# Float64 clamp on GpSimd and a shifted order of weight narrowing in a fused attention, rational layer and soft mixture kernel

## The chip, the cores and the metric

The kernel runs on one core of a Trainium2 chip, in one launch. The metric is the device time of an execution in microseconds (us). TensorE (PE) multiplies matrices; VectorE (DVE), ScalarE (ACT) and GpSimd (POOL) work elementwise; SyncE (SP) starts most of the transfers.

## The reference

Three layers follow each other. Attention works in chunks of 32 queries that see 16 keys to the left, 8 to the right and 8 memory slots. Its result, 3072 tokens by 512, goes through a rational layer and then through a soft mixture of 8 experts with 4 slots each:

```python
def _moe_ref(x, w_in, w_out, a, b):
    h = x @ w_in                                   # 512 -> 2048
    P = a[0] + a[1]*h + a[2]*h**2 + a[3]*h**3
    Q = 1.0 + abs(b[0])*abs(h) + abs(b[1])*h**2
    return (P / (Q + 1e-06)) @ w_out               # 2048 -> 512

def _moe2_ref(x, phi, w1, w2):
    logits = x @ phi                               # 32 slots
    d = softmax of logits over the tokens
    slot_out = relu((d.T @ x) @ w1[e]) @ w2[e]     # for each expert
    c = softmax of logits over the slots
    return c @ slot_out
```

The weights w_in and w_out arrive as float64 and are narrowed to float32 on the chip.

## The kernel before

The tokens are taken in six blocks of 512, and the 2048 hidden columns in eight steps of 256, so there are 48 steps, numbered k. In step k PE makes h for step k+1 (`h_part`, L380): in block 0 with plain float32 matmuls, later with a split of both operands into two parts. The elementwise chain of a step is: ACT takes |h| (L607) and h squared (L608) from PSUM, DVE adds them to the denominator Q (L609), ACT makes a3*h + a2 (L610), DVE goes on to the cubic with two passes that read h from PSUM (L619, L620). ACT makes 1/Q approximately by Ln and Exp (L624, L625). One step later POOL multiplies Q with this reciprocal (`refine`, L585), and DVE closes the Newton correction (L632, L633). The product is written into a buffer that L609 of the later step has just read, so it starts behind that L609. The result is turned on PE (L405) and multiplied with a small matrix wp (L398) to get the logits; copies are made by ACT (L406).

wp is phi times w_out, and it is made from eight pieces of w_out transposed, one per step: `narrow_w_turned` narrows piece i, `wp_sum` multiplies it (PE L483, ACT L485, PE L488, ACT L489). w_in comes in eight pieces also, narrowed by `narrow_w_in`. Pieces lie in buffers of the pool "g" (four buffers, shared with the gathered results `gts` of a block), so a load waits until an older piece was narrowed. `f64_narrow` does one piece of 128 x 1024 words in four passes: ACT scales the low words (L303), DVE clamps the high words (L304), ACT scales them (L305), DVE merges both (L307). All sixteen pieces are narrowed in the prologue and in block 0. `narrow_rows` does the same for other rows of w_out in later blocks with code of its own.

What order rules: in the prologue (up to `start.close()`) the order of PE, ACT, DVE and POOL is that of the list `pre`. After that a planner orders each engine's instructions by the order of writing, by its costs and by when their inputs are due; the list `ord0` gives the order of writing in a step of block 0, `ord` in later blocks. In the lists "s" narrows a w_in piece, "n" a w_out piece, "z" is `wp_sum`, "i" and "o" load pieces, "at" is a slice of the next block's attention, and the digit is the distance from the step's number. `issue_after(x)` keeps the planner from putting what it encloses ahead of x on x's engine; it waits for nothing.

Of the kernel before, what the change touches and what calls it, by code (L numbers as in the profile page):

```python
# [12 lines left out]
AF = mybir.ActivationFunctionType  # L13
ALU = mybir.AluOpType
# [5 lines left out]
def float_of_bits(u):  # L20
    return struct.unpack('<f', struct.pack('<I', u))[0]


KN = {
    'loads': "q0 q1 v0 i0 v1 c0 i1 o0 q2 v2 o1".split(),
    'pre': "f10 A A f5 B B A A A A B B A A B B A A A A s B B B B A A f2 A B B A s A B B A f2 B s B B B c f4 t t n n".split(),
    'pre2': "i2 o2 i3".split(),
    'ord0': "at a1 z0 s2 h0 d1 at t o3 i4 n1 at a2 y h1 p0 at p1 at at".split(),
    'ord': "at a1 h0 d1 at t a2 y x2 h1 p0 p1 x1 at x3 at at r".split(),
    'ordl': "a1 h0 d1 t a2 x2 h1 p0 p1 x1 x3 r".split(),  # L30
}

# [14 lines left out]
def tile_chunk_attention__rational__soft_moe(  # L47
# [16 lines left out]
    PE, ACT, DVE, POOL, SP = nc.tensor, nc.scalar, nc.vector, nc.gpsimd, nc.sync  # L64

    NPAIR, P, HP, _ = qw.shape
# [5 lines left out]
    NE, _, EFF = w1.shape  # L72
# [8 lines left out]
    NSTEP = NF // 2  # L81
# [4 lines left out]
    QC = 1.0 + 1e-6  # L86
    LN_SHIFT = 52
    LOW = 7.4 / 2.0 ** 32
    F64_HI = float_of_bits((1150 << 20) | 0xFFFFF)
# [22 lines left out]
    def bank(shape):  # L112
        return ps_m("m", shape)
# [160 lines left out]
    def constants():  # L274
        ACT.activation(ctab[:, 4:6], ctab[:, 4:6], AF.Abs)
        root, over = ctab[:, 7:8], run[:, 0:1]
        DVE.tensor_scalar(root, ctab[:, 5:6], 1e-37, None, ALU.max)
        ACT.activation(root, root, AF.Ln)
        ACT.activation(root, root, AF.Exp, scale=0.5)
        DVE.reciprocal(over, root)  # L280
        DVE.scalar_tensor_tensor(root, over, ctab[:, 5:6], root, ALU.mult, ALU.add)
        DVE.tensor_scalar(root, root, 0.5, None, ALU.mult)
        yield
# [7 lines left out]
    a0, a1, a2, a3 = (ctab[:, n:n + 1] for n in range(4))  # L291
# [4 lines left out]
    def f64_narrow(dst, src):  # L296

        lo, hi = src[:, :, :, 0], src[:, :, :, 1]
        f = hi.bitcast(F32)
        ACT.activation(lo, lo, AF.Copy, scale=LOW)  # L303
        DVE.tensor_scalar(f, f, -F64_HI, F64_HI, ALU.max, ALU.min)  # L304
        ACT.activation(f, f, AF.Prelu, scale=2.0 ** -112, alpha=-(2.0 ** 32))  # L305
        yield
        DVE.scalar_tensor_tensor(dst, hi, 3, lo, ALU.logical_shift_left, ALU.bitwise_or)  # L307
        yield
# [3 lines left out]
    win, w_f, st = {}, {}, {}  # L312
# [7 lines left out]
    def load_w_turned(i):  # L320
        t = p_g("g", [P, NC, 2 * P, 2], U32)
        for o in (slice(0, NC // 2), slice(NC // 2, NC)):
            SP.dma_start(out=t[:, o].rearrange("p c f w -> p c (f w)"), in_=w_turned[i, :, o])
        stage_out[i] = t

    def narrow_w_in(i):
        if i < NSTEP // 2:
            t = p_win("win", [P, 1024])
        else:
            if i % 2 == 0:  # L330
                st["x"] = p_x("x", [P, 2048])
            t = st["x"][:, 1024 * (i % 2):1024 * (i % 2) + 1024]
        w_f[i] = t.rearrange("p (c f) -> p c f", c=NC)
        yield from f64_narrow(w_f[i].bitcast(U32), stage_in.pop(i))

    def split_w(i):
        f = w_f.pop(i)
        wh, wl = win[i] = [p_win("win", [P, NC, 2 * P], F32R) for _ in range(2)]
        ACT.activation(wh, f, AF.Copy)
        DVE.tensor_tensor(wl, f, wh.bitcast(F32), ALU.subtract)  # L340
# [3 lines left out]
    def narrow_w_turned(i):  # L344
        wos[i] = scratch[i % 3].rearrange("p (c f) -> p c f", c=NC)
        yield from f64_narrow(wos[i].bitcast(U32), stage_out.pop(i))

    def load_rows(i):
        rows_of[i] = p_x("x", [P, 2, DM, 2], U32)
        SP.dma_start(out=rows_of[i].rearrange("p c f w -> p c (f w)"), in_=w_out[i])  # L350
# [145 lines left out]
    def load(what):  # L496
# [12 lines left out]
        elif kind == "o":  # L509
            load_w_turned(n)  # L510

    def convert(what):
        kind, n = what[0], int(what[1])
        if n < NSTEP:
            for _ in {"s": narrow_w_in, "n": narrow_w_turned, "z": wp_sum, "i": load_w_in, "o": load_w_turned}[kind](n) or ():
                pass

    new_xt(0)
    for what in KN["loads"]:
        load(what)  # L520
    gens = {"A": attention(0, after=NPAIR), "B": attention(1, lambda shape: p_T("T", shape), after=NPAIR),
            "s": narrow_w_in(0), "n": narrow_w_turned(0), "t": narrow_w_in(1), "c": constants()}
    for what in KN["pre"]:
        if what[0] == "f":
            busy(int(what[1:]))
# [16 lines left out]
    def slice_(n=1):  # L542
        for _ in range(n):
            if state["att"] is not None:
                try:
                    next(state["att"])
                except StopIteration:
                    state["att"] = None
# [33 lines left out]
    def refine(k, out=None):  # L582
        t, q, w = late[k]
        near[k] = out = q if out is None else out
        POOL.tensor_tensor(out, q, w, ALU.mult)  # L585

    late, near, behind, narrowing = {}, {}, {}, {}
    act = {}
# [1 line left out]
    def run_step(kk, what):  # L590
        b, i = divmod(kk, NSTEP)
        live, nxt = kk < total, kk + 1
        pb_, pi_ = divmod(kk - NSTEP, NSTEP)
        if what == "at":
            slice_()
        elif what in ("h0", "h1"):
            if nxt < total:
                if what == "h0":
                    if nxt % NSTEP == 0:
                        while state["att"] is not None:  # L600
                            slice_()
                    hs[nxt] = ps_h("h", [P, 2, BLK]) if nxt < total - 1 else [ps_h("h", [P, BLK]), bank([P, BLK])]
                h_part(nxt, hs[nxt], int(what[1]))
        elif what == "a1" and live:
            hh = hs[kk]
            s, t, y = p_S("S", [P, 2, BLK]), p_T("T", [P, 2, BLK]), p_S("S", [P, 2, BLK])
            ACT.activation(s, hh, AF.Abs, scale=b0)  # L607
            ACT.activation(y, hh, AF.Square, scale=rb1)  # L608
            DVE.scalar_tensor_tensor(s, y, QC, s, ALU.add, ALU.add)  # L609
            ACT.activation(t, hh, AF.Identity, bias=a2, scale=a3)  # L610
            act[kk] = s, t, y
        elif what == "d1":
            if live:
                s, t, y = act[kk]
                hh = hs.pop(kk)
            if kk - 1 in late and kk - 1 not in near:
                refine(kk - 1, y if nxt < total else None)
            if live:
                DVE.tensor_tensor(t, t, hh, ALU.mult)  # L619
                behind[kk] = DVE.scalar_tensor_tensor(t, t, a1, hh, ALU.add, ALU.mult).ins  # L620
        elif what == "a2" and live:
            s, t, _ = act.pop(kk)
            w = p_S("S", [P, 2, BLK])
            ACT.activation(w, s, AF.Ln, scale=2.0 ** -LN_SHIFT)  # L624
            st["exp"] = ACT.activation(w, w, AF.Exp, bias=ex_b, scale=-1.0).ins  # L625
            late[kk] = t, s, w
        elif what == "t":
            if kk - 1 in late:
                t, q, w = late.pop(kk - 1)
                e = near.pop(kk - 1)  # L630
                with tc.issue_after(behind[kk]) if kk in behind else nullcontext():
                    DVE.scalar_tensor_tensor(t, t, a0, w, ALU.add, ALU.mult)  # L632
                    st["t"] = DVE.scalar_tensor_tensor(t, e, 2.0, t, ALU.subtract, ALU.mult, reverse0=True).ins  # L633
                gt_tile[kk - 1] = t
        elif what == "y":
            if 0 <= kk - 6 < NSTEP:
                with tc.issue_after(st["exp"]):
                    split_w(kk - 6)
        elif what == "r":
            for n, at in ROWS.items():  # L640
                if kk == at[0]:
                    load_rows(n)
                    narrowing[n] = narrow_rows(n)
                for m in at[1:]:
                    if kk == m:
                        next(narrowing[n])
        elif what[0] == "x":
            n = int(what[1])
            if kk >= NSTEP and pi_ == (1, 2, 2)[n - 1]:
                (soft1, soft2, soft3)[n - 1](pb_)  # L650
        elif what[0] == "p":
            for k in LATER[i]:
                if 0 <= kk - k < total:
                    post(kk - k, int(what[1]))
        elif b == 0 and what[0] in "snwzio" and len(what) == 2:
            convert(what[0] + str(min(i + int(what[1]), NSTEP)))
# [56 lines left out]
    for kk in range(total + 4):  # L713
        b, i = divmod(kk, NSTEP)
# [138 lines left out]
    for b in range(NBLK):  # L853
        for half in range(2):
# [11 lines left out]
            for m in range(2):  # L866
                n = TT * b + 2 * half + m
# [67 lines left out]
```

## Time and profile before

| | us |
|---|---|
| median of 3 runs | 577.9 |
| lowest and highest | 576.36 and 578.36 |
| the profiled execution | 577.91 |
| its span in the trace | 575.8 |

The median is read against itself: runs differ by some 2 us. The profiled execution is as long as the median, and its span leaves out 2.1 us around it. All times in the trace count from the span's start. The prologue reaches to about 31 us, block 0 from the first L607 at 38.68 to the ninth at 133.26, the other five blocks to about 500 us, and the experts and the output fill the rest.

### The profile page before, as it was taken

How to read it: one execution, taken by the hardware profiler on the slowest of the kernel's cores; microseconds unless marked ns; L12 is line 12 of the kernel's file. 1: busy time of each engine (PE TensorE's matmuls, PEld its weight loads, DVE VectorE, ACT ScalarE, POOL GpSimd, SP SyncE). 2: the span in 40 equal slices, each digit the busy share in tenths (PEclk: the TensorE clock that was granted, in tenths of full speed). 3: DMA queues.
4: the chain of work that ended last, by engine and by line, in shares of the span. 5: the costliest groups of instructions: out<-in, count | busy, mean ns of one | idle time of the engine just before them, and what ended most of it. 6: DMA issues, size and time to landing. Idle time of an engine off the chain costs nothing.

```text
span 575.8 us, 13647 instructions
## 1 busy us (share of the span) xinstructions
PE 540.6 (94%) x5874; PEld 362.1 (63%) x5874; DVE 456.3 (79%) x572; ACT 427.9 (74%) x551; POOL 122.2 (21%) x66
## 2 busy tenths in 40 slices
PE   6799897999999999999999999999999999999991
PEld 6644443557767767677766777776768767643351
DVE  3759988989898999979899799898898978831042
ACT  1489896897978999779787888896888978721132
POOL 0001111213221322313231313132223322300000
PEclk8799898999999999999999999999999999999996
DMA  8997854301125315341432335304349374799948
GB/s 319 361 382 256 279 189 162 137 12 56 56 76 183 129 56 183 115 170 36 161 111 74 114 107 184 110 12 174 110 145 372 106 252 150 268 392 410 409 173 357
DMA packets 28139, 105.80 MB, mean 184 GB/s; under 512 B 3376, under 2 KB 3504, under 8 KB 27056
## 3 DMA queue, kind: packets, MB, share of 16 engines
q1 hardware_dynamic: 26928, 100.74, 48.1%
q0 software_dynamic: 1152, 4.19, 1.8%
q8 instruction: 46, 0.75, 0.5%
q14 instruction: 13, 0.11, 0.0%
HBM read 94.44 MB, written 10.49 MB: 182 GB/s over the span
## 4 chain that ended last, share of the span: by engine, by line
PE 56%; DVE 15%; ACT 14%; DMA 8%; issue 4%; POOL 1%; ACTq 0%; SPq 0%; DVEq 0%; POOLq 0%
PE h L380 28%; DMA g<-in_w_turned_dram 5%; PE m L405 4%; PE m L458 4%; ACT S L607 3%; PE lg L398 3%; ACT S L608 3%; ACT g L406 3%; DVE T L619 3%; PE h L796 2%; PE m L228 2%; DVE T L620 2%; PE lg L833 2%; DMA g<-in_moe_w_in_dram 2%; DVE T L632 2%
## 5 line engine op out<-in xcount | busy, mean ns | idle before, releaser
L380 PE MATMUL h<-xt,win 128*128 128x512 f32 x1012 | 268.5, 414 | 0.7 <-DVE T L620 0.6
L380 PEld LDWEIGHTS h<-xt,win 128*128 128x128 f32 x1012 | 184.1, 188 | 50.9 <-issue 12.3
L585 POOL TENSOR_TENSOR S<-S,S 128x1024 f32<-128x1024 f32 x46 | 112.2, 2440 | 335.1 <-DVE S L609 282.1
L607 ACT ACTIVATE S<-h,ctab 128x1024 f32<-128x1024 f32 x47 | 52.5, 1117 | 38.3 <-PE h L380 37.5
L609 DVE SCALAR_TENSOR_TENSOR S<-S,S 128x1024 f32<-128x1024 f32 x47 | 57.3, 1220 | 24.3 <-ACT S L608 23.7
L619 DVE TENSOR_TENSOR T<-T,h 128x1024 f32<-128x1024 f32 x47 | 57.1, 1215 | 7.6 <-ACT T L610 7.6
L405 PEld LDWEIGHTS m<-ident,T 128*128 128x128 f32 x384 | 43.4, 141 | 29.4 <-issue 14.0
L620 DVE SCALAR_TENSOR_TENSOR T<-T,ctab,h 128x1024 f32<-128x1024 f32 x47 | 59.9, 1274 | 0.7
L632 DVE SCALAR_TENSOR_TENSOR T<-T,ctab,S 128x1024 f32<-128x1024 f32 x46 | 58.6, 1274 | 0.0
L633 DVE SCALAR_TENSOR_TENSOR T<-S,T 128x1024 f32<-128x1024 f32 x46 | 56.1, 1220 | 2.4 <-DVE T L632 0.5
L406 ACT ACTIVATE g<-m 128x512 f32<-128x512 f32 x96 | 53.2, 601 | 6.3 <-PE m L405 6.0
L610 ACT ACTIVATE T<-h,ctab 128x1024 f32<-128x1024 f32 x47 | 57.5, 1223 | 0.0
L625 ACT ACTIVATE S<-S,ctab 128x1024 f32<-128x1024 f32 x47 | 54.5, 1159 | 0.9
L624 ACT ACTIVATE S<-S 128x1024 f32<-128x1024 f32 x47 | 50.5, 1074 | 6.1 <-DVE S L609 6.1
L405 PE MATMUL m<-ident,T 128*128 128x128 f32 x384 | 53.0, 278 | 1.2 <-DVE a L189 1.2
L608 ACT ACTIVATE S<-h,ctab 128x1024 f32<-128x1024 f32 x47 | 52.7, 1121 | 0.9 <-DVE T L632 0.9
L380 PE MATMUL h<-xt,x 128*128 128x512 f32 x64 | 31.4, 621 | 3.6 <-DVE x L307 3.6
L398 PE MATMUL lg<-T,wp 128*32 128x512 f32 x192 | 33.1, 605 | 1.3 <-DVE T L633 0.7
L190 ACT ACTIVATE a<-a 128x512 f32<-128x512 f32 x22 | 13.4, 639 | 16.6 <-DVE a L189 16.6
L458 PE MATMUL m<-g,s 128*32 128x512 f32 x192 | 21.8, 595 | 0.4 <-ACT s L450 0.4
L303 ACT ACTIVATE g<-g 128x1024 uint32<-128x1024 uint32 x16 | 18.7, 1166 | 4.3 <-DMA g<-in_w_turned_dram 4.3
L380 PEld LDWEIGHTS h<-xt,x 128*128 128x128 f32 x64 | 11.2, 191 | 16.3 <-issue 15.1
(218 smaller groups left out, 673.5 us busy)
## 6 DMA issues: line engine op xcount, KB each, us to landing
win<-in_moe_w_dram SPq DMA_DIRECT2D x31, 512.0 KB, 7.3
k<-in_kw_dram SPq DMA_DIRECT2D x22, 512.0 KB, 6.3
v<-in_vw_dram SPq DMA_DIRECT2D x22, 512.0 KB, 5.2
g<-in_moe_w_in_dram SPq DMA_DIRECT2D x16, 512.0 KB, 7.3
g<-in_w_turned_dram SPq DMA_DIRECT2D x16, 512.0 KB, 6.5
x<-in_moe_w_out_dram SPq DMA_DIRECT2D x8, 1024.0 KB, 4.8
out_dram<-win SPq DMA_DIRECT2D x12, 512.0 KB, 5.0
q<-in_qw_dram SPq DMA_DIRECT2D x11, 512.0 KB, 3.8
```

The lines of the kernel that those rows point to most:

```text
L380: PE.matmul(tile_[f2] if step == total - 1 else tile_[:, f2, :], lhsT=ww[:, c, f2 * P:f2 * P + P], rhs=xx[:, c, :], start=(n == 0), stop=( ...
L405: st["turn"] = PE.transpose(pb[:, m, f2 * P:f2 * P + P], t_[:, f2, tt * P:tt * P + P], ident)
L406: ACT.activation(gts[b, qd][:, 2 * part:2 * part + 2, 2 * P * o:2 * P * o + 2 * P], pb, AF.Copy)
L585: POOL.tensor_tensor(out, q, w, ALU.mult)
L607: ACT.activation(s, hh, AF.Abs, scale=b0)
L608: ACT.activation(y, hh, AF.Square, scale=rb1)
L609: DVE.scalar_tensor_tensor(s, y, QC, s, ALU.add, ALU.add)
L610: ACT.activation(t, hh, AF.Identity, bias=a2, scale=a3)
L619: DVE.tensor_tensor(t, t, hh, ALU.mult)
L620: behind[kk] = DVE.scalar_tensor_tensor(t, t, a1, hh, ALU.add, ALU.mult).ins
L632: DVE.scalar_tensor_tensor(t, t, a0, w, ALU.add, ALU.mult)
L633: st["t"] = DVE.scalar_tensor_tensor(t, e, 2.0, t, ALU.subtract, ALU.mult, reverse0=True).ins
```

## The change

Four things change. In `f64_narrow` the clamp of the high words goes from DVE to POOL as soon as a product of `refine` has been written, and is queued behind the last of these. `convert` encloses the narrowing passes of a step, so that those on DVE stay behind that step's L609 and those on ACT behind its L610. The lists change: the prologue narrows w_in pieces 0, 1 and 2 (before: w_in 0 and 1, w_out 0), step k narrows w_in k+3 (before k+2) and w_out k (before k+1), and `wp_sum` of piece k-1 stands at the head of step k, up to step 8 (before: of piece k, behind the first passes of step k). The loads follow the same shift.

```diff
-    'loads': "q0 q1 v0 i0 v1 c0 i1 o0 q2 v2 o1".split(),
-    'pre': "f10 A A f5 B B A A A A B B A A B B A A A A s B B B B A A f2 A B B A s A B B A f2 B s B B B c f4 t t n n".split(),
-    'pre2': "i2 o2 i3".split(),
-    'ord0': "at a1 z0 s2 h0 d1 at t o3 i4 n1 at a2 y h1 p0 at p1 at at".split(),
-    'ord': "at a1 h0 d1 at t a2 y x2 h1 p0 p1 x1 at x3 at at r".split(),
+    'loads': "q0 q1 v0 i0 v1 c0 i1 i2 q2 o0 v2 i3".split(),
+    'pre': "f10 A A f5 B B A A A A B B A A B B A A A A s B B B B A A f2 A B B A s t A B B t A f2 B B B B c f4 u u".split(),
+    'pre2': "i4 o1".split(),
+    'ord0': "Z at a1 s3 h0 d1 at t i5 at a2 y n0 h1 p0 o2 at p1 at at".split(),
+    'ord': "Z at a1 h0 d1 at t a2 y x2 h1 p0 p1 x1 at x3 at at r".split(),
...
         f = hi.bitcast(F32)
+        with tc.issue_after(st["q"]) if "q" in st else nullcontext():
+            (POOL if "q" in st else DVE).tensor_scalar(f, f, -F64_HI, F64_HI, ALU.max, ALU.min)
         ACT.activation(lo, lo, AF.Copy, scale=LOW)
-        DVE.tensor_scalar(f, f, -F64_HI, F64_HI, ALU.max, ALU.min)
         ACT.activation(f, f, AF.Prelu, scale=2.0 ** -112, alpha=-(2.0 ** 32))
...
+    pins = {}
+
     def convert(what):
         kind, n = what[0], int(what[1])
         if n < NSTEP:
-            for _ in {"s": narrow_w_in, "n": narrow_w_turned, "z": wp_sum, "i": load_w_in, "o": load_w_turned}[kind](n) or ():
-                pass
+            with tc.issue_after(pins[0]) if pins else nullcontext(), tc.issue_after(pins[1]) if pins else nullcontext():
+                for _ in {"s": narrow_w_in, "n": narrow_w_turned, "z": wp_sum, "i": load_w_in, "o": load_w_turned}[kind](n) or ():
+                    pass
...
-            "s": narrow_w_in(0), "n": narrow_w_turned(0), "t": narrow_w_in(1), "c": constants()}
+            "s": narrow_w_in(0), "t": narrow_w_in(1), "u": narrow_w_in(2), "c": constants()}
...
-        POOL.tensor_tensor(out, q, w, ALU.mult)
+        st["q"] = POOL.tensor_tensor(out, q, w, ALU.mult).ins
...
-            DVE.scalar_tensor_tensor(s, y, QC, s, ALU.add, ALU.add)
-            ACT.activation(t, hh, AF.Identity, bias=a2, scale=a3)
+            pins[0] = DVE.scalar_tensor_tensor(s, y, QC, s, ALU.add, ALU.add).ins
+            pins[1] = ACT.activation(t, hh, AF.Identity, bias=a2, scale=a3).ins
...
+        elif what == "Z":
+            if 0 < kk <= NSTEP:
+                convert("z" + str(kk - 1))
```

## Rows read from the trace of the kernel before

**Rows 1.** The page: busy time of PE; granted clock in 40 slices, in tenths.
```profile
PE 540.6 (94%) x5874; PEld 362.1 (63%) x5874; DVE 456.3 (79%) x572; ACT 427.9 (74%) x551; POOL 122.2 (21%) x66
PEclk8799898999999999999999999999999999999996
```

**Rows 2.** Busy time by stage: length, each engine's us (instructions), clock, DMA share, GB/s.
```profile
38.68:133.26 94.58, 86.13 (x772) 44.47 (x768) 85.41 (x95) 84.61 (x107) 18.39 (x7) 0.96 0.50 174
133.26:500.00 366.74, 362.87 (x3863) 263.75 (x3856) 328.51 (x383) 310.34 (x391) 101.57 (x50) 1.00 0.38 134
```

**Rows 3.** The same view, steps 1, 2, 4 and 5 of block 0.
```profile
49.32:58.84 9.52, 9.51 (x100) 4.91 (x92) 8.55 (x11) 9.52 (x14) 2.40 (x1) 1.00 0.86 321
58.84:74.32 15.48, 13.33 (x135) 6.73 (x136) 14.29 (x17) 13.37 (x17) 2.69 (x1) 0.89 0.79 273
...
84.26:96.97 12.71, 9.85 (x36) 3.94 (x31) 10.78 (x17) 9.29 (x12) 2.38 (x1) 1.00 0.68 236
96.97:114.25 17.28, 15.35 (x188) 8.52 (x189) 16.26 (x18) 14.42 (x22) 3.42 (x1) 0.90 0.27 95
```

**Rows 4.** Timeline of PE: start, us, operation, count, [idle before and its releaser].
```profile
62.90 0.64 PE L483 MATMUL m<-win,u 128*32 128x256 f32 x8 [1.92 <-DVE win L307]
63.47 3.62 PE L380 MATMUL h<-xt,win 128*128 128x512 f32 x4
...
97.66 1.92 PE L380 MATMUL h<-xt,x 128*128 128x512 f32 x2 [3.56 <-DVE x L307]
...
101.33 1.98 PE L380 MATMUL h<-xt,x 128*128 128x512 f32 x4
```

**Rows 5.** Timeline of ACT in step 4.
```profile
90.88 1.18 ACT L303 ACTIVATE g<-g 128x1024 uint32<-128x1024 uint32 x1 [3.42 <-DMA g<-in_w_turned_dram]
```

**Rows 6.** Groups by line, 38.68 to 133.26: busy us, mean ns, idle before, releasers.
```profile
L303 ACT ACTIVATE g<-g 128x1024 uint32<-128x1024 uint32 x13 | 15.2, 1173 | 4.3 <-DMA g<-in_w_turned_dram 4.3
L305 ACT ACTIVATE g<-g 128x1024 f32<-128x1024 f32 x13 | 15.1, 1180 | 0.7 <-DVE g L304 0.5
...
L304 DVE TENSOR_SCALAR g<-g 128x1024 f32<-128x1024 f32 x12 | 11.5, 962 | 1.5 <-DMA g<-in_moe_w_in_dram 1.5
...
L609 DVE SCALAR_TENSOR_TENSOR S<-S,S 128x1024 f32<-128x1024 f32 x8 | 9.7, 1217 | 2.9 <-ACT S L608 2.8
```

**Rows 7.** Timeline of PE and ACT at the end of h(0).
```profile
34.51 3.17 PE L380 MATMUL h<-xt,win 128*128 128x512 f32 x7
...
37.56 1.23 ACT L303 ACTIVATE g<-g 128x1024 uint32<-128x1024 uint32 x1 [0.85 <-DMA g<-in_w_turned_dram]
```

**Rows 8.** One line's instructions (L304, L307): shortest, median and longest ns.
```profile
L304 DVE TENSOR_SCALAR g<-g x16: 662/690/2872, 19.9 to 116.7; 128x1024 f32<-128x1024 f32 x16
...
L307 DVE SCALAR_TENSOR_TENSOR win<-g x12: 1211/1225/2599, 23.7 to 121.6; 128x1024 uint32<-128x1024 uint32 x12
```

**Rows 9.** Groups of POOL, whole span: busy us, mean ns, idle before.
```profile
L760 POOL MEMSET wp<- 128x512 f32 x1 | 0.5, 528 | 6.4 <-PE lg L398 6.4
...
masks.py:199 POOL TENSOR_SCALAR_AFFINE_SELECT ident<-ident 128x128 f32<-128x128 f32 x1 | 0.3, 295 | 0.1
...
L290 POOL MEMSET ctab<- 128x1 f32 x1 | 0.1, 99 | 0.0
```

**Rows 10.** Timeline of POOL and DVE where the two meet.
```profile
54.32 2.40 POOL L585 TENSOR_TENSOR S<-S,S 128x1024 f32<-128x1024 f32 x1 [52.97 <-DMA g<-in_moe_w_in_dram]
...
55.23 2.60 DVE L307 SCALAR_TENSOR_TENSOR win<-g 128x1024 uint32<-128x1024 uint32 x1
...
103.48 3.42 POOL L585 TENSOR_TENSOR S<-S,S 128x1024 f32<-128x1024 f32 x1 [10.23 <-DVE S L609]
...
104.58 2.87 DVE L304 TENSOR_SCALAR g<-g 128x1024 f32<-128x1024 f32 x1
```

**Rows 11.** Timeline of POOL and DVE in step 7.
```profile
130.10 2.42 POOL L585 TENSOR_TENSOR S<-S,S 128x1024 f32<-128x1024 f32 x1 [8.12 <-DVE S L609]
...
132.32 1.28 DVE L632 SCALAR_TENSOR_TENSOR T<-T,ctab,S 128x1024 f32<-128x1024 f32 x1
```

## The prediction

> **What bounds the kernel now.** I read first the page's busy shares and its clock line [rows 1]: TensorE (PE) is busy 94% of the span, but the clock line dips below 9 tenths in the first quarter, and nowhere later until the tail. So the change, which edits only the prologue and the eight steps of block 0, works where PE does not run unhindered. Second, the busy time by stage [rows 2], cut at two starts of the first pass of a step on ScalarE (ACT, L607): 38.68 us (step 0) and 133.26 us (step 8, block 1). In these 94.58 us PE is busy 86.13, VectorE (DVE) 85.41, ACT 84.61: three engines at 89 to 91%, each losing 8.5 to 10 us. Behind it, PE is busy 362.87 of 366.74 us at full clock. Hence a microsecond won in block 0 should move the rest forward, and nothing behind needs an edit to keep it.
>
> Third, the single steps [rows 3]. Step 1 takes 9.52 us with ACT busy throughout. Steps 2, 4 and 5 take 15.48, 12.71 and 17.28; together 45.5, so the other five share 94.6-45.5 = 49.1, 9.8 each. The three bad steps hold the loss. Fourth, PE's timeline in them [rows 4]: in step 2 PE stands 1.92 us until VectorE's merge L307 of a w_out piece feeds wp_sum's matmul L483, and the next four h matmuls take 3.62 us where four elsewhere take 1.98: about twice, so the granted clock stood at 1.2 and not 2.4 GHz after the gap (0.89 in the mean of that step [rows 3], 1.00 in step 1). In step 4 PE stands 3.56 us for the merge of the next w_in piece, and the next two matmuls take 1.92 us. Both waits hang on narrowing of float64 words (ACT L303, DVE clamp L304, ACT L305, DVE merge L307).
>
> **The change part by part.** *Passes pinned.* Before, the planner put a piece's ACT pass ahead of its step: up to 90.88 us ACT stood 3.42 us for a w_out landing, in step 4, though that piece's sum is wanted steps later [rows 5]. All such landing waits ahead of L303 are 4.3 us, and ACT waits 0.5 us more for the clamp at L305 [rows 6]. After, L303 and L305 of a step are queued behind that step's L610, L307 behind its L609. A piece is still asked for two steps, some 20 us, before its own step's pass, and only passes pulled ahead of that have waited. I book all 4.8 us of ACT's idle as gone. The price: what queues behind a pinned pass is the same step's Ln and Exp (L624, L625), moved back by two passes at most, 2.3 us by the means of L303 and L305 [rows 6]; their product is wanted only a step later, behind the next L609, so I put this at nothing; if that cover is gone, it is up to 2.3 us in a step. The slot of a piece comes free later too, and so its successor's load on SP's queue with the attention loads behind it: nothing while the two steps of lead hold.
>
> *w_out one step behind, w_in one ahead.* wp_sum's matmuls and its two ACT copies are the same, now a step after the merge; the sum for pieces 0 and 1 is wanted in step 3, so it has a step to spare. w_in for step k+3 is narrowed in step k, not k+2: the h matmuls find it finished. The count inside the 94.58 us stays 13 pieces (six w_in and seven w_out before; five and eight after), and the eighth wp_sum slips into block 1. For PE this takes away the 1.92 and 3.56 us of waiting and the slow matmuls behind them: 3.62-1.98 = 1.6 in step 2, and in step 4 some 1.9-1.0 = 0.9 for the two h matmuls, with about 0.8 on the transposes and L483 behind them (an estimate: the same relation on shorter work). Sum for PE 8.8 us. But that is what PE could give, not what the path gives: ACT's 84.6 us of work stay.
>
> *Prologue.* A second w_in piece is narrowed between the attention slices and a third behind them, in the place of w_out piece 0. ACT and DVE have holes there, and PE begins h(0) with the same inputs. Step 0's first pass starts behind a w_out pass at 37.56 that had itself waited 0.85 us for its landing, while PE had finished h(0) at 34.51+3.17 = 37.68 [rows 7]; without it the pass could begin up to 1.0 us earlier, and with the added piece in front of attention's last copies h(0) could begin up to 1.2 us later (one ACT pass [rows 6]). I take zero and keep both ends.
>
> *Clamp on GpSimd (POOL).* Thirteen clamps lie in the stretch; the 12 recorded took 11.5 us on DVE, 962 ns in the mean [rows 6] where the median one takes 690 [rows 8]. After, three (w_in 3 and 4, w_out 0: no product yet when they are written) stay on DVE, 2.1 us, and ten go to POOL. DVE's work: 85.4-11.5+2.1 = 76.0. No row shows a clamp on POOL. Per 1024 elements, the bounds are a write without a read, 2 x 0.53 = 1.05 us [rows 9], and the two-input product, 2.4 us [rows 10]; the nearest is the one-input select over 128 elements at 295 ns against 99 for one element, (0.295-0.1) x 8 + 0.1 = 1.66 [rows 9]. I take 1.5, since the fixed part is not paid twice and the clamp needs no index; ends 1.05 and 2.4.
>
> What hides it? POOL is busy 18.4 of 94.6 us [rows 2]. But the two engines exclude each other here [rows 8, 10]: DVE's merge at 55.23 took 2.60 us against a median of 1.22, ending 1.1 us after the product that ran from 54.32 to 56.72; the clamp at 104.58 took 2.87, ending just after the product of 103.48 to 106.90, and that product itself had first lasted 3.42 instead of 2.4 behind a merge. DVE's passes L619 and L620, which read PSUM for one input, run beside it undisturbed, and they are just as long as the product: in step 7 it ends at 132.52 and L632, with two inputs in SBUF, starts at 132.32 [rows 11]. A clamp queued right behind the product therefore meets L632, L633 or a merge. If all ten cost DVE their full length, that is 15 us; if none, zero. I take half, 7.5, as about half of DVE's work in a step is such two-input passes: 76.0+7.5 = 83.5.
>
> The Trainium skill, "SBUF — State Buffer", section "Who interferes with whom", says that a DVE instruction with two SBUF inputs and a GpSimd one that reads SBUF hold the port by turns, for the whole instruction; the rows above agree (2.60 and 2.87 us). Its page "GPSIMD Engine Reference", section "Engine selection", advises against GpSimd for elementwise work and calls one-input work about line rate: by that the clamp would be near 1 us, an estimate, and the sum would not change sign.
>
> **Sum.** Per engine, in the 94.58 us: PE 94.6-8.8 = 85.8; DVE 83.5 of work; ACT 94.6-4.8 = 89.8, its remaining 5.2 us of idle kept. ACT ends last, so block 0 shortens by 4.8 us. The profiled execution took 577.91 us (span 575.8 and 2.1 around it), the same as the median 577.9; the forecast is 577.9-4.8 = **573.1 us**. Next late thing: ACT's remaining waits for PE and the attention slices.
>
> **The rivals.** *Everything gained* (chance 0.20): PE's 8.8 us, since ACT's other idle mostly answers PE's gaps, and 1.0 at the first pass: 568.1. For: ACT's bare work would allow 10. Against: three engines near 90% seldom fit without gaps.
>
> *Traded waits* (0.16): the clamp's time on POOL returns to DVE as blocked merges, and pinned passes make ACT wait for the clamp: ten times 0.5 us gives back the 4.8; 578. For: the pass L305 follows the clamp directly. Against: other ACT passes lie between. That the pins do nothing, because the planner's order was already so, ends here too.
>
> *Slower by the shared port* (0.22): the clamp is as dear as the two-input product, 2.4 us, and always starts as L632 or a merge arrives. DVE then needs 76.0+24 = 100 us plus its waits for ACT's passes, of which the 2.8 us at L609 are sure [rows 6]; three quarters blocked with 5 us of waits (half of today's idle) gives 76+18+5 = 99, 4.4 more than now: 582.3. It decides from the point where blocked time goes over 94.6-76-5 = 13.6 us, that is 1.36 per clamp. For: the clamp is queued exactly behind the product. Against: the clamp of a w_in piece landed early may start under L619 or attention's passes on PSUM.
>
> **How the numbers follow.** Forecast 0.42 (571 to 575.8), all gained 0.20 (567 to 571), traded 0.16 (576 to 580), slower 0.22 (580 to 584). A measurement of this kernel can tell about 0.3%, 1.7 us, from no change. Faster 0.62, same 0.16, slower 0.22. For 8 in 10 I leave out the lowest edge and most of the slower case: 567.5 to 580.5; the forecast's own range is 571 to 575.8.
>
> **What would show each step.** Right: PE's waits for L307 in block 0 gone and no half-clock stretch between 60 and 105 us; no landing wait at L303; step 8 starting near 128.5 us; ten clamps on POOL of 1.05 to 1.7 us; the rest of the trace moved as a whole. Wrong: L632, L633, L609 or L307 lasting over 2 us beside a clamp, DVE's busy time in block 0 above 85; ACT waiting for POOL at L305; h(0) starting after 31 us; or block 1 and the tail keeping their old times although step 8 came earlier.

## The result and the profile after

The changed kernel takes 583.77 us (median of 4 runs, 583.37 to 584.98); the kernel before, 578.04 beside it. The ratio is 1.0109, with a 95% interval of 1.0084 to 1.0134: 5.7 us slower, where 4.8 us faster was forecast. The profiled execution took 584.98 us, the longest of the four, with a span of 583.2 us, 7.4 more than before. Two of the runs below (587.19 us with three idle clamps a piece, 670.63 us with the last prologue) count as slow: the medians include them, the ratios do not.

In the listing of the changed kernel the lines after the clamp have moved: L305 and L306 are now the two ACT passes of a piece (L303, L305 before), L308 the merge (L307), L589 the product (L585), L611 to L614 the first passes of a step (L607 to L610), L636 and L637 the last two on DVE (L632, L633).

The busy time by stage of the changed kernel, cut at the same first pass of ACT in steps 0 and 8, has the columns of [rows 2] (length; PE, weight loads, DVE, ACT, POOL; clock; DMA):

```profile
39.84:138.83 98.99, 86.09 (x845) 45.78 (x844) 82.43 (x88) 85.52 (x106) 58.55 (x17) 0.98 0.48 160
138.83:510.00 371.17, 362.90 (x3875) 265.27 (x3876) 329.11 (x384) 310.27 (x392) 102.06 (x50) 1.00 0.39 135
```

Block 0 takes 98.99 us instead of 94.58, though DVE has 3.0 us less to do there, PE as much as before and ACT 0.9 us more. POOL went from 18.4 to 58.6 us. So hardly anybody has more work but POOL, and everybody waits more. The first pass of step 0 is 1.2 us late; step 8 starts 5.6 us late (138.83 against 133.26), and step 12's first pass 7.2 us late (180.39 against 173.18). The difference stays at about that to the end, but it did not grow evenly (end of this section).

The groups by line of block 0, with the columns of [rows 6], show who waits:

```profile
L304 POOL TENSOR_SCALAR g<-g 128x1024 f32<-128x1024 f32 x10 | 42.1, 4228 | 0.0
...
L305 ACT ACTIVATE g<-g 128x1024 uint32<-128x1024 uint32 x13 | 15.2, 1170 | 0.0
L306 ACT ACTIVATE g<-g 128x1024 f32<-128x1024 f32 x13 | 15.0, 1156 | 11.3 <-POOL g L304 10.3 <-DVE g L304 1.1
L308 DVE SCALAR_TENSOR_TENSOR win<-g 128x1024 uint32<-128x1024 uint32 x9 | 10.9, 1211 | 8.2 <-ACT g L306 8.2
L636 DVE SCALAR_TENSOR_TENSOR T<-T,ctab,S 128x1024 f32<-128x1024 f32 x7 | 10.3, 1466 | 0.0
...
L484 PE MATMUL m<-win,u 128*32 128x256 f32 x56 | 4.5, 391 | 3.5 <-DVE win L308 3.5
```

A clamp on POOL lasts 4.2 us in the mean. ACT's landing waits of 4.3 us are gone, as forecast, and 10.3 us of waits for the clamp stand in their place. DVE then waits 8.2 us for ACT at the merge, and PE 3.5 us for the merge. The timeline of step 2 and the start of step 3 shows the chain once (start, us, operation, [idle before and its releaser]):

```profile
66.40 2.38 POOL L589 TENSOR_TENSOR S<-S,S 128x1024 f32<-128x1024 f32 x1 [2.22 <-DVE S L613]
68.75 8.50 POOL L304 TENSOR_SCALAR g<-g 128x1024 f32<-128x1024 f32 x2
...
73.53 1.13 ACT L306 ACTIVATE g<-g 128x1024 f32<-128x1024 f32 x1 [2.06 <-POOL g L304]
...
74.70 1.23 DVE L308 SCALAR_TENSOR_TENSOR win<-g 128x1024 uint32<-128x1024 uint32 x1 [2.45 <-ACT g L306]
...
75.50 1.13 ACT L611 ACTIVATE S<-h,ctab 128x1024 f32<-128x1024 f32 x1
...
75.84 1.22 DVE L637 SCALAR_TENSOR_TENSOR T<-S,T 128x1024 f32<-128x1024 f32 x1
```

The product waits for the step's L613, the clamp for the product, ACT's L306 for the clamp, the merge for L306. Behind L306 on ACT stands L611, the first pass of step 3; behind the merge on DVE stands L637, which closes the step's correction. Both queues are in order, so a clamp that ends late holds up passes that have nothing to do with it.

Of the 7.2 us, a part arises behind block 0. Near 150 us PE is only 2.4 us late, at the same logits matmuls. First the kernel before, then the changed one:

```profile
149.75 1.07 PE L398 MATMUL lg<-T,wp 128*32 128x512 f32 x8
...
151.75 1.88 PE L380 MATMUL h<-xt,win 128*128 128x512 f32 x7
```

```profile
152.16 1.06 PE L399 MATMUL lg<-T,wp 128*32 128x512 f32 x8
...
154.47 1.11 ACT L611 ACTIVATE S<-h,ctab 128x1024 f32<-128x1024 f32 x1 [1.47 <-POOL S L589]
155.48 1.14 ACT L629 ACTIVATE S<-S,ctab 128x1024 f32<-128x1024 f32 x1
156.52 1.04 ACT L340 ACTIVATE win<-win 128x1024 fp32r<-128x1024 f32 x1
157.62 2.77 PE L381 MATMUL h<-xt,win 128*128 128x512 f32 x7 [3.38 <-ACT win L340]
```

PE waits 3.38 us for L340, which makes the first of the two parts of a w_in piece for block 1, and the seven matmuls behind the wait take 2.77 instead of 1.88 us (the granted clock is 0.89 in the mean from 154.47 to 170.16, so after PE had stood still part of the stretch ran at 1.2 and not 2.4 GHz). ACT has step 10's first pass, L611, ahead of step 9's Exp (L629) and of L340, and L611 had itself waited 1.47 us for POOL's product; before, Exp and split stood ahead of the first pass. No clamp runs there: the last one ended at 136.84. A wait of PE of 2.1 to 3.4 us stands at this place in every profile of a kernel with the new lists, but for the two that have clamps on POOL and no pins, and in none with the old lists.

### The profile page after: what moved, and what is told of

Its sections match the earlier page's. It is cut to its first block, busy times and chain, and to the rows that moved or that the text cites. A ratio compares the mean times of both kernels' runs of the same rounds, so it can differ in the third digit from the quotient of the medians.

```text
span 583.2 us, 13655 instructions
## 1 busy us (share of the span) xinstructions
PE 536.0 (92%) x5874; PEld 360.8 (62%) x5874; DVE 451.0 (77%) x562; ACT 427.3 (73%) x551; POOL 162.4 (28%) x76
## 4 chain that ended last, share of the span: by engine, by line
PE 49%; DVE 17%; ACT 13%; POOL 7%; DMA 6%; issue 6%; SPq 0%; ACTq 0%; POOLq 0%; DVEq 0%
PE h L381 25%; PE m L406 4%; POOL g L304 4%; PE m L459 4%; DMA win<-in_moe_w_dram 3%; ACT S L611 3%; PE lg L399 3%; ACT S L612 3%; DVE S L613 3%; POOL S L589 3%; PE m L228 2%; DVE T L624 2%; DVE T L623 2%; ACT g L407 2%; DMA T<-in_moe_w_dram 2%
## 5 line engine op out<-in xcount | busy, mean ns | idle before, releaser
L589 POOL TENSOR_TENSOR S<-S,S 128x1024 f32<-128x1024 f32 x46 | 110.5, 2402 | 302.1 <-DVE S L613 250.5
L611 ACT ACTIVATE S<-h,ctab 128x1024 f32<-128x1024 f32 x47 | 52.5, 1117 | 40.7 <-PE h L381 38.5
L613 DVE SCALAR_TENSOR_TENSOR S<-S,S 128x1024 f32<-128x1024 f32 x47 | 57.3, 1218 | 32.2 <-ACT S L612 31.8
L636 DVE SCALAR_TENSOR_TENSOR T<-T,ctab,S 128x1024 f32<-128x1024 f32 x46 | 59.9, 1302 | 0.0
L637 DVE SCALAR_TENSOR_TENSOR T<-S,T 128x1024 f32<-128x1024 f32 x46 | 56.9, 1237 | 2.2
L614 ACT ACTIVATE T<-h,ctab 128x1024 f32<-128x1024 f32 x47 | 57.6, 1225 | 0.0
L629 ACT ACTIVATE S<-S,ctab 128x1024 f32<-128x1024 f32 x47 | 54.4, 1157 | 0.8
L304 POOL TENSOR_SCALAR g<-g 128x1024 f32<-128x1024 f32 x10 | 42.1, 4228 | 0.0
L306 ACT ACTIVATE g<-g 128x1024 f32<-128x1024 f32 x16 | 18.5, 1156 | 12.4 <-POOL g L304 10.3
```

Of the source, the lines that this page charges most:

```text
L304: (POOL if "q" in st else DVE).tensor_scalar(f, f, -F64_HI, F64_HI, ALU.max, ALU.min)
L589: st["q"] = POOL.tensor_tensor(out, q, w, ALU.mult).ins
L613: pins[0] = DVE.scalar_tensor_tensor(s, y, QC, s, ALU.add, ALU.add).ins
L614: pins[1] = ACT.activation(t, hh, AF.Identity, bias=a2, scale=a3).ins
```

## Experiments

The theories: 1, the clamp on POOL costs; 2, the new order of the pieces costs; 3, the pins cost. Within the first: 1a, as a link of the chain just shown; 1b, by keeping POOL and its port busy. Where a kernel differs from the change or from the kernel before, its diff is against that one. The kernel before took 577.4 to 577.6 us beside each group of runs, and 578.04 beside the change, so the medians can be compared to about half a microsecond.

### One part at a time

**Everything but the clamp's move.** All clamps stay on DVE; the rest is the change.

```diff
-        with tc.issue_after(st["q"]) if "q" in st else nullcontext():
-            (POOL if "q" in st else DVE).tensor_scalar(f, f, -F64_HI, F64_HI, ALU.max, ALU.min)
+        DVE.tensor_scalar(f, f, -F64_HI, F64_HI, ALU.max, ALU.min)
```

> The whole change but for one thing: every clamp stays on DVE. Theory 1, the clamp on POOL (3.8 to 4.8 us each in the changed kernel, in the line product, clamp, L305, merge) is what costs: ACT's 10.3 us of waits for POOL go, and the time falls to 572 to 577 us. Theory 2, the new order of the pieces costs (the last w_out piece now narrowed in step 7, the third w_in piece in the prologue): 581 us or more. Theory 3, the pins cost (L305 stands at ACT's head with the next step's passes behind it): about 580 us, as the pins remain.

Measured: 574.81 us, ratio 0.9954 (0.9933 to 0.9975). So 9.0 us of the changed kernel's 583.77 hang on where the clamp runs, and without it the change is faster than before. Its block 0:

```profile
39.58:130.01 90.43, 86.32 (x846) 45.46 (x845) 86.58 (x97) 85.91 (x106) 18.13 (x7) 1.00 0.52 178
```

It takes 90.43 us, 4.2 less than before, near the 89.8 of the forecast, and the granted clock is 1.00 in the mean. Less of that arrives behind it: after waits for splits (1.32 and 2.23 us), step 12's first pass is 0.8 us earlier than before (172.34 against 173.18), in a profiled execution of 576.63 us.

**The clamp's move alone**, in the kernel before.

```diff
+        with tc.issue_after(st["q"]) if "q" in st else nullcontext():
+            (POOL if "q" in st else DVE).tensor_scalar(f, f, -F64_HI, F64_HI, ALU.max, ALU.min)
         ACT.activation(lo, lo, AF.Copy, scale=LOW)
-        DVE.tensor_scalar(f, f, -F64_HI, F64_HI, ALU.max, ALU.min)
...
-        POOL.tensor_tensor(out, q, w, ALU.mult)
+        st["q"] = POOL.tensor_tensor(out, q, w, ALU.mult).ins
```

> The kernel before with nothing but the clamp moved to POOL behind its product (ten clamps, no pins, the old order of the pieces). Theory 1: each clamp lasts 3.8 us or more, merges come later, PE waits for them: 582 to 588 us. Theories 2 and 3: within 2 us of the kernel before (578).

Measured: 592.32 us, ratio 1.0265 (1.0218 to 1.0312): 14.7 us slower, more than any theory had asked for. Theory 1 stands, and the other parts of the change must soften the clamp's cost.

**The pins alone**, in the kernel before.

```diff
...
+            with tc.issue_after(pins[0]) if pins else nullcontext(), tc.issue_after(pins[1]) if pins else nullcontext():
...
+            pins[0] = DVE.scalar_tensor_tensor(s, y, QC, s, ALU.add, ALU.add).ins
+            pins[1] = ACT.activation(t, hh, AF.Identity, bias=a2, scale=a3).ins
```

> The kernel before with nothing but the pins: passes of ACT behind L610 of their step, of DVE behind L609. Theory 1: the 4.3 us of landing waits at L303 go, 574 to 578 us. Theory 3: 581 us or more, since PE then waits longer for the merges of its own step.

Measured: 579.73 us, ratio 1.0041 (1.0023 to 1.0060): 2.2 us slower, between the two expectations. The groups of the whole span show why it is not faster (the columns as above):

```profile
L303 ACT ACTIVATE g<-g 128x1024 uint32<-128x1024 uint32 x16 | 18.4, 1173 | 0.0
...
L380 PE MATMUL h<-xt,x 128*128 128x512 f32 x64 | 33.1, 642 | 5.3 <-DVE x L307 5.1 <-DVE T L623 0.2
```

The 4.3 us of landing waits are gone from L303, and PE now waits 5.1 us for the merge of a w_in piece, where it had waited 3.6 [rows 4]. This fits a piece that, narrowed only two steps ahead, comes too late once its passes may not move forward. The kernel did not gain by the end of the landing waits; whether they cost anything by themselves, this run cannot tell, as it changed both.

**The lists alone**: the change without the clamp's move and without the pins.

```diff
-            (POOL if "q" in st else DVE).tensor_scalar(f, f, -F64_HI, F64_HI, ALU.max, ALU.min)
+        DVE.tensor_scalar(f, f, -F64_HI, F64_HI, ALU.max, ALU.min)
...
-            with tc.issue_after(pins[0]) if pins else nullcontext(), tc.issue_after(pins[1]) if pins else nullcontext():
...
```

> The kernel before with nothing but the new lists: w_in narrowed one step earlier, w_out one later, wp_sum at the head of the next step, the prologue with w_in 0 to 2; clamps on DVE, no pins. Theory 1: PE's waits of 1.92 and 3.56 us for merges go, 572 to 577 us. Theory 2: 581 us or more; the first pass of step 0 starts at 39.8 instead of 38.7 us in any case, if the prologue's order is the cause of that.

Measured: 573.75 us, ratio 0.9936 (0.9904 to 0.9967). The whole gain, 3.8 us, lies in the lists; theory 2 falls. ACT's landing waits are gone here too, without pins (0.2 us of idle are left ahead of that pass). PE no longer waits for a w_in merge at all:

```profile
L380 PE MATMUL h<-xt,x 128*128 128x512 f32 x64 | 31.0, 607 | 0.0
...
L483 PE MATMUL m<-win,u 128*32 128x256 f32 x64 | 5.6, 420 | 3.4 <-DVE win L307 3.4
```

Its wait at wp_sum stays, 3.4 us, in spite of the step in between. The difference to lists and pins together (574.81) is smaller than the two intervals.

**Lists and clamp without the pins**: the change less the same lines as in the run before.

> The changed kernel without the pins: clamps on POOL and the new lists. Theory 1 with pins of little weight (2 us, as alone): 581 to 586 us, like the changed kernel. If the pins soften the clamp's cost (passes pulled ahead wait at the head of ACT for POOL): 588 us or more, since clamp alone cost 14.7 us and clamp with lists and pins 9.0.

Measured: 590.53 us, ratio 1.0243 (1.0197 to 1.0289). This is above the 588 us that stood for pins that soften the clamp's cost: they save 6.8 us when the clamp is on POOL. ACT's pass behind the clamp, the group of the whole span, in this kernel:

```profile
L306 ACT ACTIVATE g<-g 128x1024 f32<-128x1024 f32 x16 | 18.3, 1145 | 24.4 <-POOL g L304 22.9 <-DVE g L304 1.4
```

The same group in the kernel with the clamp's move alone:

```profile
L306 ACT ACTIVATE g<-g 128x1024 f32<-128x1024 f32 x16 | 18.4, 1156 | 25.0 <-POOL g L304 23.1 <-DVE g L304 1.9
```

And in the changed kernel:

```profile
L306 ACT ACTIVATE g<-g 128x1024 f32<-128x1024 f32 x16 | 18.5, 1156 | 12.4 <-POOL g L304 10.3 <-DVE g L304 2.1
```

ACT waits 22.9, 23.1 and 10.3 us for the clamp, and moving it to POOL costs 16.8 (590.53 less 573.75), 14.7 and 9.0 us. Waits and costs both set the kernels without pins apart from the one with them; between the first two the order is not the same. Without pins L306 often stands ahead of the step's Ln or Exp in ACT's queue (in the run of this section at 59.34 us, after 4.84 us of waiting, with Exp behind it), where in the timeline of the changed kernel it stands behind both (they start at 68.34 and 70.33), and ACT waits longer.

### Link of the chain or occupied engine

**The clamp a step ahead.** The clamps stay on POOL behind the product, but each is written one step before the other three passes of its piece. Nine go to POOL, since w_out piece 1 now comes before the first product.

```diff
-    'ord0': "Z at a1 s3 h0 d1 at t i5 at a2 y n0 h1 p0 o2 at p1 at at".split(),
+    'ord0': "Z at a1 s3 h0 d1 S4 N1 at t i5 at a2 y n0 h1 p0 o2 at p1 at at".split(),
...
             (POOL if "q" in st else DVE).tensor_scalar(f, f, -F64_HI, F64_HI, ALU.max, ALU.min)
+        if st.pop("early", None):
+            yield
...
```

> The whole change, with the ten clamps still on POOL behind the product, but each written a step ahead of the other three passes of its piece, so that no pass of ACT or DVE has to wait for it. POOL is as busy as in the changed kernel. Theory 1a, the clamp costs as a link of the chain (L305 waits at ACT's head, the merge at DVE's): 573 to 577 us, like the change with clamps on DVE (574.8). Theory 1b, it costs by occupying POOL and the port: 581 us or more, like the changed kernel (583.8).

Measured: 574.38 us, ratio 0.9964 (0.9936 to 0.9991). Its clamps and the pass behind them, whole span:

```profile
L304 POOL TENSOR_SCALAR g<-g 128x1024 f32<-128x1024 f32 x9 | 38.1, 4271 | 0.6 <-DMA g<-in_w_turned_dram 0.6
...
L308 ACT ACTIVATE g<-g 128x1024 f32<-128x1024 f32 x16 | 18.6, 1162 | 1.1 <-DVE g L304 1.1
```

The clamps are as long as in the change, 4.3 us, but ACT never waits for POOL, and 9.4 us come back (583.77 less 574.38). That is theory 1a, though DVE has fewer clamps here than in the kernel with all of them on it.

**The clamp ahead of the product.** The change without the order that keeps the clamp behind the product.

```diff
-        with tc.issue_after(st["q"]) if "q" in st else nullcontext():
+        with nullcontext():
             (POOL if "q" in st else DVE).tensor_scalar(f, f, -F64_HI, F64_HI, ALU.max, ALU.min)
```

> The changed kernel without the order behind the product: the planner is free, and puts each pair of clamps ahead of the product of its step instead of behind it. If the place behind the product (2.4 us later) is what makes ACT wait for the clamp: ACT's 10.3 us of waits fall, 576 to 580 us. If the clamp's own 3.8 us are enough, the waits stay or the product is late instead: 582 to 586 us.

Measured: 577.26 us, ratio 0.9987 (0.9965 to 1.0009). ACT does not wait for POOL here either:

```profile
L306 ACT ACTIVATE g<-g 128x1024 f32<-128x1024 f32 x16 | 18.7, 1167 | 1.0 <-DVE g L304 1.0
```

So 6.5 of the 9.0 us hang on one edge, the one that puts the clamp behind a product that itself waits for the step's L613. The 2.5 us that are left over the kernel with clamps on DVE agree with late products (step 2's starts at 68.44 us, with clamps on DVE at 66.12), but no run isolates them.

**Idle clamps beside the real ones.** All real clamps on DVE, and for each that the change moved, clamps on POOL of a buffer that nobody reads at that time. First three of 128 x 320 words, then two of 128 x 500 in a row (only the second is shown).

```diff
+        if "q" in st:
+            with tc.issue_after(st["q"]):
+                for _ in range(2):
+                    POOL.tensor_scalar(beside, beside, -F64_HI, F64_HI, ALU.max, ALU.min)
```

> The whole change with every real clamp on DVE, and beside each clamp that the change put on POOL three clamps of 128 x 320 words of a buffer that nobody reads at that time, in the same place on POOL behind the product: POOL is as busy as in the changed kernel (some 3.8 us per piece), but nobody waits for the result. Theory 1a, the clamp costs as a link of the chain (ACT's L305 and DVE's merge wait for it, with the next step's passes behind them in their queues): at most 1.5 us over the same kernel without them, 574 to 577 us. Theory 1b, it costs by occupying POOL and the port (later products, blocked DVE passes): 580 to 584 us, as the changed kernel.

Measured: 582.29 us, with runs from 577.8 to 587.2, ratio 1.0079 (1.0039 to 1.0120). Three such passes took 5.1 to 6.2 us, so that POOL with two pieces in a step had hardly any room left, and this in the fastest of the ten executions, which is the profiled one: the run told more of a full POOL than of the change.

> As the run with idle clamps beside the real ones, but with 2 x 500 words in a row per piece, near 3.8 us by the prices measured in the prologue; the three of 320 words took 5.1 to 6 us and overfilled POOL in steps 2 to 4 (2.4 us and twice 5.5 in steps of 11 to 13 us). Theory 1a: 574 to 577 us. Theory 1b: 581 us or more.

Measured: 578.52 us, ratio 1.0012 (0.9987 to 1.0037), 3.7 us over the same kernel without them and between the two expectations. So theory 1b has a share: a POOL that is as busy, for 4.1 to 5.4 us a piece, costs 3.7 us where nobody waits for its result. With the real clamps a step ahead, DVE is rid of nine clamps at the same time; that the two about cancel there (574.38 against 574.81) is a reading, and no run takes them apart.

**Early clamps without pins**: the kernel with clamps a step ahead, less the pins.

> The new lists, clamps on POOL written a step ahead of the other passes, and no pins. Theory 1a: with pins this form took 574.4, and pins alone cost 2.2 us, so 571 to 574 us, at or under the lists alone (573.75). If the pins are what makes the early clamp harmless (a pass pulled ahead of its step finds the clamp unfinished, as in the run without pins, where ACT waited 22.9 us for POOL): 578 us or more.

Measured: 574.22 us, ratio 0.9950 (0.9933 to 0.9967). ACT waits 5.7 us for POOL, far from 22.9, and the time is that of the pinned form, a little above the 571 to 574 that were expected. Three kernels now beat both the kernel before and the change, and no interval tells them apart: lists alone (573.75), this one, and early clamps with pins (574.38). The traces do. At the logits matmuls that the kernel before starts at 149.75 us PE is 5.8, 2.7 and 7.0 us ahead of it (143.92, 147.06 and 142.80); at the matmuls of its L458, at 162.78, it is 4.0, 2.7 and 4.2 us ahead (158.82, 160.11 and 158.55). The first and the last lose 1.9 and 2.7 us in between, where PE waits 2.2 and 2.9 us; this one has no such wait. A kernel with the lead of the last and the order of this one in block 1 was not tried.

### What a clamp costs, and the prologue

**Prices on POOL.** The kernel before, with nine passes on a buffer of their own while POOL is idle.

> The kernel before with nine extra passes on POOL in the prologue, on a buffer of their own, where POOL is idle: what a clamp costs by itself and of what. The clamp of every second word, 1024 of them, as in the change: 3.8 us. If the price is the stride (8 bytes): the same clamp of 1024 words in a row takes half or less. If it is the two operations: one operation takes half. If it is a fixed price: 512 words take nearly as long as 1024. The time of the kernel stays at 578 within 2 us.

The time of the kernel was 578.51 us. POOL's timeline, in the order written (L295 clamp of every second word, 1024 of them; L296 the same of 512; L297 clamp of 1024 in a row; L298 and L299 one operation instead of two, every second word and in a row; L300 a product of two stretches in a row; L302 a fill):

```profile
3.19 3.77 POOL L295 TENSOR_SCALAR x<-x 128x1024 f32<-128x1024 f32 x1
7.04 2.02 POOL L296 TENSOR_SCALAR x<-x 128x512 f32<-128x512 f32 x1
9.14 3.62 POOL L297 TENSOR_SCALAR x<-x 128x1024 f32<-128x1024 f32 x1
12.85 2.91 POOL L298 TENSOR_SCALAR x<-x 128x1024 f32<-128x1024 f32 x1
15.84 2.76 POOL L299 TENSOR_SCALAR x<-x 128x1024 f32<-128x1024 f32 x1
18.68 2.37 POOL L300 TENSOR_TENSOR x<-x 128x1024 f32<-128x1024 f32 x1
...
23.09 1.01 POOL L302 MEMSET x<- 128x1024 f32 x1
```

The stride is worth 0.15 us and the fixed part 0.27 (2 x 2.02 less 3.77). The second operation costs 0.86 us; one operation with a constant, 2.76 us, already costs more than a product of two tensors.

**The prologue.** The lists alone, with both further w_in pieces narrowed behind the attention slices.

```diff
-    'pre': "f10 A A f5 B B A A A A B B A A B B A A A A s B B B B A A f2 A B B A s t A B B t A f2 B B B B c f4 u u".split(),
+    'pre': "f10 A A f5 B B A A A A B B A A B B A A A A s B B B B A A f2 A B B A s A B B A f2 B s B B B c f4 t t u u".split(),
```

> The new lists without clamp and pins (573.75 us), but with the prologue's w_in pieces 1 and 2 both narrowed behind the attention slices, as before the change; the loads keep their new order. If the passes between the slices delay h(0) (31.8 to 32.7 us in the kernels with the new prologue, 30.5 to 31.2 in those with the old one), it starts by 31.2 and the time falls by about 1 us, to 572.5. If the order of the loads delays it, it stays at 32 us and the time at 573.8.

Measured: 575.62 us, ratio 0.9976 (0.9954 to 0.9997), no gain over 573.75. Its profiled execution is the one of 670.63 us, so its h(0) at 31.60 us says little. In the other kernels h(0) starts at 30.91 to 32.67 us with the new prologue and at 30.54 to 31.21 with the old one, the kernel with the nine extra passes aside: the ranges overlap, and what moves it stays open. In the change it started at 32.67, 2.1 us later than before. In the kernel with the extra passes it started at 34.26 and step 0's first pass at 41.43, 2.75 us late, and its only run took 578.51 us: a hint, no more, that a late start is not paid for in full.

## Why the prediction was wrong

- **What bounds block 0** was read rightly. With clamps on DVE the stretch fell from 94.58 to 90.43 us; the forecast had 89.8, and 573.1 us for the whole, where lists with pins gave 574.8 and lists alone 573.75. Not so the sentence that nothing behind block 0 needs an edit to keep a gain: with lists alone 1.9 of 5.8 us were lost again near 150 us.
- **Pins**: the landing waits at L303 went, as forecast, but the step "I book all 4.8 us of ACT's idle as gone" was not a gain. Pins alone took the same waits away and cost 2.2 us, and the lists alone took them away as well. This speaks for ACT's idle as a symptom. What the lists removed was PE's wait for the w_in merge, 3.6 us to none; that the 3.8 us which they gave are near that is in part luck, as the wait at wp_sum grew from 1.9 to 3.4 us and the one in block 1 is new. The claim that both of PE's waits go held for w_in only: at wp_sum 3.4 us remained in the lists alone.
- **The clamp's price** is the first step that failed. The text took 1.5 us, with ends of 1.05 and 2.4, from a fill, a select and the two-input product. Alone it takes 3.77 us, in block 0 4.2. The upper end was a product of two tensors, 2.4 us; no row showed that a pass with one input is cheaper, and on POOL one operation with a constant already takes 2.76 us and the second another 0.86.
- **What the price falls on** is the second. The text asked only how long DVE would be blocked, and took 7.5 us. DVE's busy time came out at 82.43 against the 83.5 of the sum, but that is in part luck: blocking beside clamps was small (L636 rose from 1279 to 1466 ns in block 0), while one of the three clamps left on DVE took 2.56 us beside a product and the stretch holds two passes more than before, seven L637 for six and two L341 for one. Instead ACT waited 10.3 us for the clamp. "Traded waits" named this wait and waved it off with "other ACT passes lie between"; with product and clamp in series, 2.4 + 4.2 us behind L613, they do not cover it. At 3.8 us the wait at L306 should have been priced from the clamp's end, and with it what stands behind L306 on ACT and behind the merge on DVE.
- **"Slower by the shared port"** gave 582.3 us and the right sign, and that the time came near it is luck, as the mechanism was another: DVE was not the engine that ran over. A busy POOL has a share (3.7 us with idle clamps), offset by what DVE is spared.
- **The prologue** was taken as zero, with 1.2 us as its late end; in the profiled execution h(0) came 2.1 us later, and step 0's first pass 1.2. What this cost is not known.
- **The rest of the trace** did not move as a whole at step 8. ACT's first pass was 5.6 us late there, PE at the logits matmuls near 150 us 2.4, and the wait for L340 with the slow matmuls behind it made it 7.2, where it stayed. The prediction has no term for this wait. Which of the lists' shifts puts ACT's order so was not tried.

## What to carry to other kernels

Before a pass is moved to an engine with room, price the same form of pass on that engine, and if no row shows it, do not cap its price with a different operation. Then ask when its result is due, not only whom it blocks: a pass that sits in series between two in-order queues delays everything queued behind its consumers, and an order edge behind a late producer adds that producer's lateness. If it must move, start it a step earlier; here that returned all of the 9 us that its move had cost. And read the stretch behind the edit as well: a lead can be lost at a wait that was not there before.

## What the runs showed of the hardware

A clamp with two constants on GpSimd, 128 x 1024 float32 words, takes 3.77 us on every second word and 3.62 in a row, and one operation with a constant 2.91 and 2.76, against 2.37 us for a product of two tensors in a row and 0.69 us for the clamp on VectorE [rows 8].

The port rule did not hold for the clamp as it does for the product. Beside the product, a DVE pass with two SBUF inputs waited until its end [rows 10]. Beside two clamps in the changed kernel (55.33 to 64.18 us), the same kind of pass ran in 1.59 and 1.23 us against medians near 1.28 and 1.22:

```profile
55.33 8.85 POOL L304 TENSOR_SCALAR g<-g 128x1024 f32<-128x1024 f32 x2
...
60.98 1.59 DVE L636 SCALAR_TENSOR_TENSOR T<-T,ctab,S 128x1024 f32<-128x1024 f32 x1
...
62.69 1.23 DVE L637 SCALAR_TENSOR_TENSOR T<-S,T 128x1024 f32<-128x1024 f32 x1
```

The longest such passes beside a clamp in block 0 took 2.21 and 1.98 us (at 82.94 and 133.29) and still ended before it did. The clamps stretched, to 4.2 us in the mean and 4.82 at most. The Trainium skill, "SBUF — State Buffer", section "Who interferes with whom", would have the later of the two wait for the whole of the other; these rows disagree for a one-input clamp on GpSimd and agree for the product. The 2.87 us that the prediction names beside that rule are a clamp on DVE, which has one SBUF input and so is no case of two.
